# A planner's slack behind DMA landings, eight shifts in its order, and a last store from ScalarE's queue

## The chip, the cores and the metric

The kernel runs on one core of one Trainium2 chip. The time is device microseconds of one execution, and the median over repeated executions is compared. A core has five engines with instruction streams of their own: TensorE (PE, with its weight loads shown apart as PEld), VectorE (DVE), ScalarE (ACT), GpSimd (POOL) and SyncE (SP). SyncE only issues DMAs here. Engines wait for each other, and for DMAs, through semaphores.

## The reference

Two layers, each an attention block and a feed-forward block, over 2048 tokens of width 640 in bfloat16, applied twice with the same weights. The attention has 32 heads of width 20 and works in four segments of 512 tokens: softmax attention inside the segment, and a linear read from a memory `M`, `z` that earlier segments have written.

```python
for s in range(N):                       # N = 4 segments of L = 512
    logits = einsum('bhqd,bhkd->bhqk', qs, ks) * scale + mask
    a_dot = einsum('bhqk,bhkd->bhqd', softmax(logits), vs)
    pq = phi(qs)                         # t + 1 where t > 0, else exp(t)
    a_mem = einsum('bhld,bhde->bhle', pq, M) / (einsum('bhld,bhd->bhl', pq, z) + 1e-6)
    outs.append(g * a_mem + (1 - g) * a_dot)
    M, z = M + einsum('bhld,bhle->bhde', phi(ks), vs), z + sum(phi(ks))
...
x = x + A(layernorm(x)) ; x = x + relu(layernorm(x) @ w1) @ w2     # twice
```

The feed-forward block is 640 to 1728 and back.

## The kernel before

All of `x` stays in SBUF (`x_sb`). The work goes in eight segment passes, layer `a` 0 or 1 and segment `s` 0 to 3; pass number 4a + s is called the rank. A pass has these steps, each a Python generator that yields one instruction group at a time:

- `proj_ln`, `proj_one`, `proj_v`: layer norm, turn the rows by a DMA transpose (`xnT`), multiply with wq, wk, wv (L658, or L661 when the weight is split in four pieces of 32 columns), and evict to `stg` and `v_aug`.
- `spill` and `fill`: store `stg` to DRAM (`scr`, L946) and load it back as `pad`, four DMAs for a pair of head groups (L993), so that the 20 rows of a head stand at multiples of 32.
- `scores`, `exps`, `causal`: scores of four heads side by side (L1177), exponentials to `PT` on ScalarE (L1239), the diagonal masked on GpSimd (L1251).
- `apply`, `turn_pair`, `divide`: multiply `PT` by v (L1271), evict to `otu` (L1281), turn it by DMA to `otk`, and on VectorE divide by the sums: a reciprocal that waits for `otk` (L1357), a scaling (L1360), two products into `o_sb` (L1365).
- `phi_`, `turn_k`, `mem_write`, `mem_read`, `combine`: the memory. `phi_` is a VectorE step that waits for the landing of `scr` (L1020), an exponential on ScalarE (L1022) and a minimum on VectorE (L1023).
- `turn_o`, `out_proj`: turn `o_sb` to `oT` by two DMA transposes, multiply by wo, add to `x_sb` (L1393).
- `ln_b`, `ffn_rest`, `ffn`: layer norm, first product with ReLU (L1475 on VectorE or L1476 on ScalarE), second product, add to `x_sb` (L1497).
- `store`: write a tile of 128 tokens to the output (L1529). The last tile goes in three pieces of 320, 160 and 160 columns (L1525).

No order is written by hand. A planner, `Sched`, holds one stream per generator (39 of them, 0 to 38 in the order in which they are added, plus short ones that a stream spawns) and writes out the engines' instruction lists before the kernel is built. It has planned durations for every step and a planned landing time for every DMA. In each round it looks at the head of every stream, works out when it could start on its engine, and takes the one with the smallest key:

```python
key = (round(start + late), 0.5 if op.urgent else prio, self.rank[id(st[1])], n)
```

`start` is the planned start in ns, `n` the stream's number, and `late` an amount by which a step is put behind others. `_late` gives TensorE's steps such an amount when one of their inputs would be ready only just before their start: up to 400 ns (`SOFT`) behind another engine's result, and up to 1000 ns (`SOFT_DMA`) behind a DMA's landing. It does so only from the event `SOFT_FROM` on, a set of scores in the second segment of the first layer. Steps of the other engines had no such amount, and neither had the pairs of score groups, which pass through a class of their own (`Either`).

The planner only fixes the order on each engine and the semaphore waits that the data need. What happens on the chip follows from real durations: each of ScalarE, VectorE, GpSimd and SyncE does its list from front to back, so a step that waits holds all steps behind it. TensorE switches between three kinds of work: whole matmuls, row groups (scores) and column groups.

Of the kernel before, what the change touches and what calls it, by code (L numbers as in the profile page):

```python
# [38 lines left out]
class Prog:  # L39
    def __init__(self, sems):  # L40
        self.ops = {e: [] for e in ENGS}
        self.clk = dict(sems)
        self.cnt = {e: 0 for e in ["act", "dve", "pool", "pe"]}
        self.dcnt = {}
        self.K = {e: {} for e in ENGS}
        self.pos = {e: 0 for e in ENGS}
        self.info = {}
# [36 lines left out]
    def dma(self, e, fn, sem):  # L84
        self.pos[e] += 1
        self.dcnt[id(sem)] = self.dcnt.get(id(sem), 0) + 16
        tk = (sem, self.dcnt[id(sem)])
        self.ops[e].append(("op", fn, sem, 16))
        self.info[(id(sem), tk[1])] = ("dma%d" % id(sem), tk[1], dict(self.K[e]))
        return tk  # L90
# [71 lines left out]
        self.gen = gen  # L162


LONE_NS = 300.0
SWITCH_NS = 96.0
COLS_LAG = 1500.0
SOFT = 400
SOFT_DMA = 1000
SOFT_FROM = ("sc",6,4,1)  # L170
SEM_NS = 60.0
PE_MARGIN = 80.0
# [4 lines left out]
class Sched:  # L177


    def __init__(self, prog):  # L180
        self.P = prog
        self.free = {e: 800.0 for e in ENGS}
        self.t = {}
        self.events = {}
        self.streams = []
        self.dma_free = 0.0
        self.rank = {}
        self.mode = "full"
        self.landed = set()

    def add(self, prio, gen):
        self.streams.append([prio, gen, None, None, False])
        self.rank[id(gen)] = 0

    def at(self, tk):
# [2 lines left out]
    def set(self, *key, tks=()):  # L198
        assert key not in self.events, key
        self.events[key] = [t for t in tks if t is not None]  # L200
# [44 lines left out]
    def _alts(self, op):  # L245
# [17 lines left out]
            res.append((start + hold, start, k, e))  # L263
        return res

    def _late(self, op):
        late = 0.0
        if op.alts[0][0] == "pe" and SOFT_FROM in self.events:
            waits = op.waits
            if op.acq is not None:  # L270
                s = self._pick(op.acq)
                waits = waits + (s.tks if s is not None else [])
            start = max([self.free["pe"]] + [self.at(t) + SEM_NS + PE_MARGIN for t in waits])
            for t in waits:
                k = (id(t[0]), t[1])
                late = max(late, self.t[k] + SEM_NS + PE_MARGIN + (SOFT_DMA if k in self.landed else SOFT) - start)
        if not op.lag or self.mode != "full":
            return late
        waits = op.waits
        if op.acq is not None:  # L280
            s = self._pick(op.acq)
            waits = waits + (s.tks if s is not None else [])
        ready = max([self.at(t) for t in waits], default=0.0) + SEM_NS + PE_MARGIN
        return max(late, ready + op.lag - max(ready, self.free["pe"]))

    def run(self):
        while True:
            best = None
            moved = True
            while moved:  # L290
                moved = False
                for st in list(self.streams):
                    had, ended = st[2], st[4]
                    self._settle(st)
                    moved = moved or st[4] != ended
                    moved = moved or st[2] is not had
            heads = []
            for n, st in enumerate(self.streams):
                if st[4]:
                    continue  # L300
                if isinstance(st[2], Op):
                    heads.append((st[0], n, st, self._alts(st[2]), st[2], self._late(st[2])))
                elif isinstance(st[2], Either):
                    both, lone = st[2].fn()
                    if both is not None:
                        heads.append((st[0], n, st, self._alts(both), both, 0.0))
                    if lone is not None:
                        heads.append((8, n, st, self._alts(lone), lone, LONE_NS))
            for prio, n, st, alts, op, late in heads:
                ok = []  # L310
                for end, start, k, e in alts:
                    if not any(p2 < min(prio, HOLDERS) and st2 is not st
                               and any(e2 == e and s2 + HOLD_TOL[e] < end for _, s2, _, e2 in al2[:1])
                               for p2, _, st2, al2, _, _ in heads):
                        ok.append((end, start, k))
                if not ok:
                    continue
                end, start, k = min(ok)
                key = (round(start + late), 0.5 if op.urgent else prio, self.rank[id(st[1])], n)
                if best is None or key < best[0]:  # L320
                    best = (key, st, end, start, k, op)
            if best is None:
                stuck = [st for st in self.streams if not st[4]]
                if not stuck:
                    return
                raise RuntimeError("stuck: " + "; ".join(
                    str(getattr(st[2], "key", None) or [s.name for s in getattr(st[2], "slots", [])][:2]) for st in stuck))
            _, st, end, start, k, op = best
            e, hold, fns, tail = op.alts[k]
            if e == "pe":  # L330
                op.mode = self._mode(op)
                self.mode = op.mode
                if op.mode == "cols" and op.cols is not None:
                    fns = op.cols
            waits, slot = op.waits, None
            for s in op.take:
                s.free = False
            if op.acq is not None:
                slot = self._pick(op.acq)
                slot.free = False  # L340
                waits = waits + slot.tks
                fns = [(lambda eng, fn=fn, slot=slot: fn(eng, slot), mark) for fn, mark in fns]
            self.P.waits(e, waits)
            self.free[e] = end
            if op.dma is not None:
                tk = self.P.dma(e, fns[0][0], op.dma)
                self.landed.add((id(tk[0]), tk[1]))
                self.dma_free = max(self.dma_free, start + 300.0) + tail[1]
                self.t[(id(tk[0]), tk[1])] = max(self.dma_free, end) + tail[0]
                if tail[2]:  # L350
                    self.free[e] = max(end, self.dma_free)
                out = tk
            else:
                marks = []
                for fn, mark in fns:
                    tk = self.P.op(e, fn, mark)
                    if tk is not None:
                        self.t[(id(tk[0]), tk[1])] = end + tail
                        marks.append(tk)
                out = marks[0] if len(marks) == 1 else (marks or None)  # L360
            st[2], st[3] = None, ((slot, out) if slot is not None else out,)
# [52 lines left out]
def bass_interleave_layers__memory_aug_infini_attn__dense_activation_relu__prompt_kernel(  # L414
    nc, A_x, A_wq, A_wk, A_wv, A_wo, A_beta, B_x, B_w1, B_w2, out,
):
    with contextlib.ExitStack() as es:
# [3 lines left out]
        S = Sched(P)  # L421
# [1095 lines left out]
        def store(b, s):  # L1517
            if b == 0:
                return
            for i in range(NJ):  # L1520
                t = 4 * s + i
                if (s, i) == (NSEG - 1, NJ - 1):
                    for hf, c0, n in ((0, 0, 320), (1, 320, 160), (2, 480, 160)):
                        tks = yield Need("sum", b, s, 2 * i + hf)
                        S.last = yield dma("sp", dout, 256 * n, lambda e, c0=c0, n=n: e.dma_start(  # L1525
                            out[0, t * 128:(t + 1) * 128, c0:c0 + n], x_sb[:, t, c0:c0 + n]), tks)
                    return
                tks = yield Need("xB", b, s, i)
                S.last = yield dma("sp", dout, 163840, lambda e, t=t: e.dma_start(  # L1529
                    out[0, t * 128:(t + 1) * 128, :], x_sb[:, t, :]), tks)  # L1530

        dout = sem_("d_out")
# [48 lines left out]
        S.add(6, each(ffn))  # L1581
        S.add(5, each(ffn_rest))
        S.add(6, each(store))
        S.add(7, warm_pe())
        S.add(7, consts())
# [35 lines left out]
```

The softmax here doesn't subtract the row's maximum and nothing guards it: scores larger than these inputs give would overflow.

## Time and profile before

| what | us |
|---|---|
| median of 10 runs | 559.28 |
| lowest and highest of them | 557.94, 561.74 |
| the profiled execution | 561.83 |
| its span, first to last instruction | 559.9 |
| ScalarE busy | 405.8 |
| VectorE busy | 416.7 |
| GpSimd busy | 191.8 |
| exponentials L1239, 320 of them, mean 1027 ns | 309.1 |

The span is what the trace covers; the execution's own time holds some 1.9 us more around it. The profile splits the time three ways: busy time of each engine, groups of instructions by line with the idle time of the engine in front of them and what ended it, and the chain of waits, which follows the end of the run back to what released each step. The granted TensorE clock is full throughout. DMAs move 61.3 MB in all, most on SyncE's queue; each also ends in a wait of some engine, and from issue to landing the turned rows `otk` take 3.4 us in the median, `xnT` 3.8, `oT` 3.6.

### The profile page before, as it was taken

The page shows a single profiled execution, that of the slowest core. Times are in us where ns is not written, and L with a number is a line of the kernel's source. Part 1 is how long each engine was busy: PE and PEld are TensorE (multiplying, and loading weights), DVE is VectorE, ACT ScalarE, POOL GpSimd, SP SyncE. Part 2 cuts the span into 40 slices and gives each one's busy share as a digit, 9 for nine tenths or more (in the row PEclk, how much of TensorE's full clock was granted, in tenths as well). Part 3 has the DMA queues.
Part 4 walks back from the last instruction along what each step waited for, and adds up shares of the span by engine and source line. Part 5 has one row for each costly group of instructions (what it writes and reads, how often), then busy time and mean ns, then how long its engine had stood idle before and what let it go on. Part 6 is the DMA issues. An engine that isn't in the chain of part 4 may idle for free.

```text
span 559.9 us, 18928 instructions
## 1 busy us (share of the span) xinstructions
PE 547.0 (98%) x8265; PEld 308.7 (55%) x8265; DVE 416.7 (74%) x1063; ACT 405.8 (72%) x514; POOL 191.8 (34%) x302
## 2 busy tenths in 40 slices
PE   8998999999999999999999999999999999999997
PEld 7454654455554555646446554565555654666656
DVE  4967988898899798897779988889965767335102
ACT  5699889899777887797788887887865787432140
POOL 5245344333344334344433443335410433201000
PEclk9999999999999999999999999999999999999999
DMA  8595999925684148275285423872426412443101
GB/s 270 133 229 155 223 192 205 235 50 78 112 162 83 38 100 168 55 102 100 59 186 99 91 44 108 155 127 21 67 56 167 108 45 29 89 84 61 40 2 50
DMA packets 130292, 61.32 MB, mean 110 GB/s; under 512 B 109090, under 2 KB 120098, under 8 KB 130210
## 3 DMA queue, kind: packets, MB, share of 16 engines
q1 hardware_dynamic: 129792, 59.62, 49.9%
q8 instruction: 65, 1.06, 0.8%
q10 hardware_dynamic: 418, 0.49, 0.3%
q14 instruction: 17, 0.14, 0.1%
HBM read 20.57 MB, written 12.85 MB: 60 GB/s over the span
## 4 chain that ended last, share of the span: by engine, by line
PE 82%; DMA 7%; DVE 7%; ACT 2%; SPq 1%; issue 1%; POOL 0%; ACTq 0%; POOLq 0%
PE ps L658 39%; PE ps L661 24%; PE ps L1177 8%; PE ps L1271 6%; DMA otk<-otu 4%; ACT PT L1239 2%; PE ps L1310 1%; PE ps L1114 1%; PE ps L1057 1%; PE ps L635 1%; DMA xnT<-xn_tok 1%; DVE o_sb L1365 1%; DMA phk<-phs 1%; PE ps L1451 1%; DMA pad<-scr 1%
## 5 line engine op out<-in xcount | busy, mean ns | idle before, releaser
L1239 ACT ACTIVATE PT<-ps 128x1024 bf16<-128x1024 f32 x320 | 309.1, 1027 | 66.3 <-PE ps L1177 62.0
L1251 POOL TENSOR_SCALAR_AFFINE_SELECT PT<-PT 128x512 bf16<-128x512 bf16 x256 | 166.1, 666 | 268.1 <-ACT PT L1239 267.9
L658 PE MATMUL ps<-w_r,hT 128*128 128x320 bf16 x508 | 81.5, 299 | 0.0
L1497 DVE TENSOR_TENSOR x_sb<-x_sb,ps 128x320 bf16<-128x320 bf16 (+1 forms) x65 | 30.8, 474 | 55.0 <-PE ps L661 45.7
L661 PE MATMUL ps<-xnT,w_r 128*32 128x512 bf16 x1144 | 68.3, 379 | 0.5 <-issue 0.5
L1177 PE MATMUL ps<-pad 20*128 20x512 bf16 (+3 forms) x1024 | 63.4, 301 | 3.0 <-ACT PT L1239 2.1
L658 PEld LDWEIGHTS ps<-w_r,hT 128*128 128x128 bf16 x508 | 47.4, 98 | 23.7 <-issue 5.3
L658 PE MATMUL ps<-xnT,w_r 128*128 128x512 bf16 x234 | 57.9, 380 | 1.3 <-DVE hT L1475 0.9
L679 DVE BATCH_NORM_STATS2 stats<-x_sb 128x6 f32<-128x320 bf16 x124 | 55.5, 469 | 2.9 <-DMA x_sb<-in_A_x_dram 2.5
L1476 ACT ACTIVATE hT<-ps 128x512 bf16<-128x512 f32 x57 | 34.1, 599 | 23.4 <-PE ps L661 20.8
L661 PE MATMUL ps<-w_r,hT 128*32 128x320 bf16 (+1 forms) x1348 | 49.7, 294 | 0.0
L1177 PEld LDWEIGHTS ps<-pad 20*128 20x128 bf16 x1024 | 17.9, 92 | 54.6 <-issue 25.1
L661 PEld LDWEIGHTS ps<-xnT,w_r 128*32 128x32 bf16 x1144 | 29.4, 97 | 25.2 <-issue 0.7
L1281 DVE CAST otu<-ps 128x512 bf16<-128x512 f32 x51 | 34.9, 684 | 10.6 <-PE ps L1271 10.4
L1271 PE MATMUL ps<-PT,v_aug 128*21 128x128 bf16 (+3 forms) x896 | 40.5, 301 | 0.0
L661 PEld LDWEIGHTS ps<-w_r,hT 128*32 128x32 bf16 x1348 | 34.7, 97 | 8.9
L1393 DVE TENSOR_TENSOR x_sb<-x_sb,ps 128x320 bf16<-128x320 bf16 x64 | 30.0, 477 | 12.1 <-PE ps L661 8.6
L1475 DVE TENSOR_SCALAR hT<-ps 128x512 bf16<-128x512 f32 x47 | 32.2, 685 | 7.3 <-PE ps L658 5.5
L695 POOL TENSOR_TENSOR rstd<-lnU,mhalf 128x2 f32<-128x2 f32 (+2 forms) x26 | 20.6, 791 | 45.6 <-DVE lnU L691 36.0
L658 PE MATMUL ps<-wo_r,oT 128*128 128x320 bf16 x223 | 35.4, 300 | 0.4 <-DVE x_sb L1393 0.4
L658 PEld LDWEIGHTS ps<-xnT,w_r 128*128 128x128 bf16 x234 | 20.9, 97 | 25.3 <-issue 5.1
L1022 ACT ACTIVATE stg<-stg 128x512 bf16<-128x512 bf16 x50 | 31.5, 634 | 2.5 <-DVE rtmp L1020 2.2
(109 smaller groups left out, 739.6 us busy)
## 6 DMA issues: line engine op xcount, KB each, us to landing
pad<-scr SPq DMA_DIRECT2D x124, 80.0 KB
scr<-stg SPq DMA_DIRECT2D x34, 256.0 KB, 3.4
out_dram<-x_sb SPq DMA_DIRECT2D x15, 160.0 KB, 1.8
w_r<-in_B_w_dram SPq DMA_DIRECT2D x10, 216.0 KB, 2.5
w_r<-in_B_w_dram SPq DMA_DIRECT2D x13, 160.0 KB, 3.3
x_sb<-in_A_x_dram SPq DMA_DIRECT2D x10, 160.0 KB, 3.2
scr<-w_r SPq DMA_DIRECT2D x5, 256.0 KB, 3.0
wv_r<-in_A_wv_dram SPq DMA_DIRECT2D x1, 800.0 KB, 8.3
```

Of the source, the lines that this page charges most:

```text
L658: return e.matmul(view(dst.ap, b), a, b, start=(k == 0), stop=(k == last))
L661: return e.matmul(view(dst.ap[rows], b), part, b, start=(k == 0), stop=(k == last))
L679: tk = yield dve(320, 1, lambda e, c2=c2: e.bn_stats(stats6[:, t % 12, c2, :], x_sb[:, t, c2 * 320:(c2 + 1) * 320]), xt)
L1022: te = yield act(512, lambda e, q=q: e.activation(q, q, ACT.Exp), [tr] + p, psum=False)
L1177: fns.append([(lambda e, z=z, j=j, hh=hh, N=N, o=o, sl=sl, q=hh % 2: e.matmul(slot.ap[:, q, o:o + N], sl.ap[32 * hh:32 * hh + DH, z, 0, 12 ...
L1239: tx = yield act(1024, lambda e, dst=dst, src=src: e.activation(dst, src, ACT.Exp, scale=SCALE), sc + pw)
L1251: tm = yield pool(600.0, lambda e, reg=reg: e.affine_select(out=reg, in_=reg, pattern=[[0, 4], [1, 128]], compare_op=ALU.is_ge, fill=0.0, ...
L1271: fns.append((lambda e, OD, j=j, hh=hh: e.matmul(OD.ap[32 * hh:32 * hh + DH + 1, 128 * j:L], VAUG[vx(a, s)][:, j, 4 * g + hh, :], pt.ap[:, ...
L1281: te = yield evac(L, 1, lambda e: e.tensor_copy(dst, OD.ap), lambda e: e.activation(dst, OD.ap, ACT.Copy), [tk] + OTU[0].tks)
L1475: th = yield evac(512, 1, lambda e: e.tensor_scalar(hT[:, dc, :], bk.ap[:, :], 0.0, None, ALU.max), lambda e: e.activation(hT[:, dc, :], b ...
L1476: lambda e: e.activation(hT[:, dc, :], bk.ap[:, :], ACT.Relu), [tk] + HT.tks)
L1497: ta = yield dve(n, 1, lambda e: e.tensor_tensor(x_sb[:, t, c0:c0 + n], x_sb[:, t, c0:c0 + n], bk.ap[:, 0:n], ALU.add), [tk], urgent=True)
```

## The change

Four edits, all in the planner but the last.

1. `_late` now also gives an amount to steps of ScalarE, VectorE and GpSimd that are no DMAs: from `SOFT_FROM` on, a step that would start less than 1000 ns after the planned landing of a DMA it waits for is ranked as if it started at landing plus 1000 ns.
2. `_landing` does the same for pairs of score groups, behind the landing of `pad`.
3. A table `NUDGE` adds an amount in ns to the key of a stream's steps during one rank: for (stream, rank), turn_o 7, out_proj's second half 9, ln_b's second half 11, combine 14, turn_k 19, ffn_rest 33, loads 37. Ended streams are dropped from the list, so each stream now carries its number along.
4. Of the three pieces of the last tile the third is issued by ScalarE's queue instead of SyncE's.

Ranking a step later does not make it wait on the chip: it may be written behind another step in its engine's list, or stay where it was.

```diff
--- before.py
+++ after.py
@@ -162,6 +162,16 @@
         self.gen = gen
 
 
+NUDGE = {
+    (7, 2): 200,
+    (9, 2): -450,
+    (11, 5): 450,
+    (14, 2): 200,
+    (14, 7): 100,
+    (19, 6): -100,
+    (33, 2): 100,
+    (37, 0): -200,
+}
 LONE_NS = 300.0
 SWITCH_NS = 96.0
 COLS_LAG = 1500.0
@@ -183,13 +193,15 @@
         self.t = {}
         self.events = {}
         self.streams = []
+        self.count = 0
         self.dma_free = 0.0
         self.rank = {}
         self.mode = "full"
         self.landed = set()
 
     def add(self, prio, gen):
-        self.streams.append([prio, gen, None, None, False])
+        self.streams.append([prio, gen, None, None, False, self.count])
+        self.count += 1
         self.rank[id(gen)] = 0
 
     def at(self, tk):
@@ -263,6 +275,12 @@
             res.append((start + hold, start, k, e))
         return res
 
+    def _landing(self, op):
+        start = max([self.free["pe"]] + [self.at(t) + SEM_NS + PE_MARGIN for t in op.waits])
+        soft = SOFT_DMA if SOFT_FROM in self.events else 0.0
+        return max([0.0] + [self.at(t) + SEM_NS + PE_MARGIN + soft - start for t in op.waits
+                           if (id(t[0]), t[1]) in self.landed])
+
     def _late(self, op):
         late = 0.0
         if op.alts[0][0] == "pe" and SOFT_FROM in self.events:
@@ -274,6 +292,9 @@
             for t in waits:
                 k = (id(t[0]), t[1])
                 late = max(late, self.t[k] + SEM_NS + PE_MARGIN + (SOFT_DMA if k in self.landed else SOFT) - start)
+        if op.alts[0][0] != "pe" and op.dma is None and SOFT_FROM in self.events:
+            start = max([self.free[op.alts[0][0]]] + [self.at(t) + SEM_NS for t in op.waits])
+            late = max([0.0] + [self.at(t) + SEM_NS + 1000 - start for t in op.waits if (id(t[0]), t[1]) in self.landed])
         if not op.lag or self.mode != "full":
             return late
         waits = op.waits
@@ -286,6 +307,7 @@
     def run(self):
         while True:
             best = None
+            self.streams = [st for st in self.streams if not st[4]]
             moved = True
             while moved:
                 moved = False
@@ -295,7 +317,8 @@
                     moved = moved or st[4] != ended
                     moved = moved or st[2] is not had
             heads = []
-            for n, st in enumerate(self.streams):
+            for st in self.streams:
+                n = st[5]
                 if st[4]:
                     continue
                 if isinstance(st[2], Op):
@@ -303,7 +326,7 @@
                 elif isinstance(st[2], Either):
                     both, lone = st[2].fn()
                     if both is not None:
-                        heads.append((st[0], n, st, self._alts(both), both, 0.0))
+                        heads.append((st[0], n, st, self._alts(both), both, self._landing(both)))
                     if lone is not None:
                         heads.append((8, n, st, self._alts(lone), lone, LONE_NS))
             for prio, n, st, alts, op, late in heads:
@@ -316,7 +339,7 @@
                 if not ok:
                     continue
                 end, start, k = min(ok)
-                key = (round(start + late), 0.5 if op.urgent else prio, self.rank[id(st[1])], n)
+                key = (round(start + late + NUDGE.get((n, self.rank[id(st[1])]), 0)), 0.5 if op.urgent else prio, self.rank[id(st[1])], n)
                 if best is None or key < best[0]:
                     best = (key, st, end, start, k, op)
             if best is None:
@@ -1522,7 +1545,7 @@
                 if (s, i) == (NSEG - 1, NJ - 1):
                     for hf, c0, n in ((0, 0, 320), (1, 320, 160), (2, 480, 160)):
                         tks = yield Need("sum", b, s, 2 * i + hf)
-                        S.last = yield dma("sp", dout, 256 * n, lambda e, c0=c0, n=n: e.dma_start(
+                        S.last = yield dma(("sp", "sp", "act")[hf], dout, 256 * n, lambda e, c0=c0, n=n: e.dma_start(
                             out[0, t * 128:(t + 1) * 128, c0:c0 + n], x_sb[:, t, c0:c0 + n]), tks)
                     return
                 tks = yield Need("xB", b, s, i)
```

## The prediction

> **What bounds the kernel now.** I read the page's busy times and its chain first, then the table of stretches over the part whose order changes, then the weight loads in front of every pause of TensorE, then the chains that end in those pauses, and last SyncE's queue and the end.
>
> ```profile
> PE 547.0 (98%) x8265; PEld 308.7 (55%) x8265; DVE 416.7 (74%) x1063; ACT 405.8 (72%) x514; POOL 191.8 (34%) x302
> ...
> PE 82%; DMA 7%; DVE 7%; ACT 2%; SPq 1%; issue 1%; POOL 0%; ACTq 0%; POOLq 0%
> ```
>
> TensorE is the bound: busy 98% of the span, and 82% of the chain. A reordering can gain only where TensorE pauses. The instruction order of the two kernels is the same up to the 1,427th matmul, which the trace has at 119.7 us; everything before that stays. The stretches after it (columns: length, then busy time of PE, PEld, DVE, ACT, POOL, then clock, DMA share, GB/s):
>
> ```profile
> 135.00:165.00 30.00, 29.42 (x387) 16.50 (x388) 26.22 (x70) 22.13 (x25) 12.04 (x19) 1.00 0.72 129
> 165.00:200.00 35.00, 33.89 (x483) 16.57 (x471) 30.89 (x74) 28.42 (x35) 13.21 (x21) 1.00 0.33 68
> ...
> 350.00:400.00 50.00, 49.30 (x685) 27.17 (x678) 44.94 (x112) 40.41 (x51) 20.12 (x30) 1.00 0.57 98
> 400.00:430.00 30.00, 29.02 (x539) 16.41 (x537) 18.50 (x48) 18.60 (x28) 4.78 (x7) 1.00 0.41 96
> ```
>
> Length less PE: 0.58 + 1.11 + 0.70 + 0.98 = 3.4 us of pause; all other stretches from 119.9 on are full, the last 69.6 us, 487 to 556.6, among them. The modelled end of a matmul hides part of a pause, so I size each by the weight load that follows (its idle time in the bracket). Ordinary gaps there are 0.26 us before a score group and 0.23 after one:
>
> ```profile
> 148.53 0.52 PEld L658 LDWEIGHTS ps<-wo_r,oT 128*128 128x128 bf16 x5 [0.72 <-DVE x_sb L1393]
> ...
> 197.32 0.13 PEld L1177 LDWEIGHTS ps<-pad 20*128 20x128 bf16 x4 [1.15 <-issue]
> ...
> 428.18 0.10 PEld L1177 LDWEIGHTS ps<-pad 20*128 20x128 bf16 x4 [1.15 <-DMA pad<-scr]
> ```
>
> Over the ordinary gap these are 0.5, 0.9 and 0.9 us. Four more are idle 0.64 us at 153.6, 0.73 at 166.8, 1.00 at 367.9 and 0.50 at 407.1, which is 0.4, 0.5, 0.7 and 0.3 too much. Sum 4.2 us: all that a perfect order could take from this part. What starts them, at 197:
>
> ```profile
> 187.36 4.84 DMA otk<-otu
> 192.20 0.02 issue
> 192.22 0.35 DVE rden L1357
> ...
> 194.19 0.22 DVE rtmp L1020
> 194.41 0.02 issue
> 194.43 0.63 ACT stg L1022
> ```
>
> VectorE stood 1.08 us at L1357 for the turned rows `otk`; L1020 and the PSUM evictions stood behind it, ScalarE's step L1022 behind L1020, and behind that the exponentials that free the score banks (L1239, 1.83 us in the chain from 195.39). The chain to 148.5 has the same head: `otk` issued at 142.17, L1357 idle 1.28 us, then the two L1393 whose banks TensorE wants. And on SyncE:
>
> ```profile
> 420.51 2.89 SPq L701 DMA_TRANSPOSE oT<-o_sb  x2
> 423.50 1.69 SPq L993 DMA_DIRECT2D pad<-scr  x4
> ```
>
> The `pad` rows for which TensorE waits at 428.2 were issued behind 2.89 us of transposes. For the end, the line of the last three stores (shortest, median and longest issue in ns, then first and last start):
>
> ```profile
> L1525 SPq DMA_DIRECT2D out_dram<-x_sb x3: 332/332/1312, 555.2 to 557.0; - x3
> ```
>
> The first two stores took 332 ns to issue, the third 1312; the last matmul and its addition are over at 556.97, and the span ends at 559.9.
>
> **What the Trainium skill says.** "TensorE: Matmul & The Clock Gate", section "Architectural detail: the array is 16× 32×32, not 1× 128×128", says that ScalarE and VectorE work strictly in order; the chain to 197.3 agrees, one wait of 1.08 us at L1357 moved work that needs no `otk`. "TensorEngine Tiling (Array Packing)", "Key Properties", says that changing the tiling mode drains the array; the 0.26 and 0.23 us around a score group, against none inside a run, agree. "DMA: Bandwidth & Descriptors", "Issuing engines are not separate DMA queues", says that the same 16 engines carry what SyncE and ScalarE issue, and only issue time is saved. "Runtime: NRT & Kernel Launch", "Instruction fetch mechanics", has instructions fetched in 16 KiB blocks; the trace has such packets, one of 1.69 us at 556.2, under the final stores.
>
> **The change part by part.** *Work on TensorE.* I counted the new order. Eleven 512-column matmuls take 2.48 us in the chain, 0.21 each once the last one's 0.38 is off. Weighting all columns so, with four pieces of a split matmul side by side, the old order holds 489.8 us of columns and the new 489.7. Changes of mode: 334 in both. The 252 fewer matmul instructions are split groups made whole, with the same columns: nothing. So whatever is gained or lost is pauses.
>
> *Slack of 1 us for steps of VectorE, ScalarE and GpSimd behind a landing.* It adds no wait; it ranks a step that would start within 1 us of its landing's planned time behind steps that are ready. I measured the room by the columns TensorE works off between the step that an `otk` transfer comes from and the last one VectorE knows of when it reads. Over the 25 divisions in the changed part the median goes from 4.26 to 5.35 us, and those under 4.2 us from 12 to 2. VectorE's five waits at L1357 between 120 and 487 us are 4.2 us in the profile; two reached TensorE. Gone: 0.9 (197) + 0.5 (148) = 1.4 us. The others cost nothing even now, having hidden beside full PSUM banks.
>
> *The same slack for score pairs, and the table.* Score pairs are now ranked behind the landing of `pad` like other matmuls. The table moves turn_o and combine of segment 2 by +200 ns, out_proj's second half by -450, ln_b's second half of segment 5 by +450, combine of 7 by +100, turn_k of 6 by -100, ffn_rest of 2 by +100, and loads by -200 (which leaves the start as it was). These are ranks alone. What I can read off is SyncE's order: for the last segment all 16 `pad` loads now come before the `oT` pair, so the 2.89 us are no longer ahead of the one that TensorE lacked at 428: 0.9 us gone. In exchange that `oT` pair is issued later, behind loads of 0.3 to 0.4 us each. Ten ReLU evictions go from ScalarE (599 ns) to VectorE (685 ns): 6.9 us more there, covered by 143 us of idle; if the cover is gone, 0.1 us each.
>
> *The pauses left.* The one at 166.8 (0.5) hangs on `xnT`, whose least room goes from 7.05 to 6.54 us: I leave it. Those at 153.6, 368 and 407 (1.4) hang on queues of VectorE and ScalarE that are shuffled anyway; I let them be replaced by as much.
>
> *Last store from ScalarE.* ScalarE has nothing from 549 us on, so nothing is queued behind its wait. No row shows a store there; its two loads of x at the start took 392 and 443 ns to issue, its small copies 670 to 1348. Bounds: 1.0 us gained (1312 to 332), or 0.5 lost if a queue unused since 20 us starts slowly. The data still shares the engine that fetches instructions until 557.9, so I take 0.8 gained.
>
> Sum: 1.4 + 0.9 + 0.8 = 3.1 us. The profiled execution was 561.83 us (span 559.9, 1.9 around it) and would become 558.7. The median of the runs, 2.5 lower, goes from 559.28 to 556.2.
>
> **The rivals.** *More than that.* The reshuffle also clears 166.8 and the other three, and the store gains its full 1.0: 4.2 + 1.0 = 5.2, giving 554.1. For it: the stretches 200 to 350 show that this loop can run with no pause. Against: nothing in the slack addresses a pause without a DMA in its chain.
>
> *As before.* The slack works on planned times, and the plan's error is what made the pauses; new ones of some 2.5 us turn up elsewhere, and the store gains 0.3: 559.0. For it: three of five waits at L1357 were hidden, so removing waits need not move TensorE.
>
> *Slower.* Dividing later makes a segment's last `o_sb` later, and with it `oT` and the output projection. Place: the seven handovers from L1365 to L658 on `oT` in the changed part. In columns their least room goes from 6.70 to 6.28 us, and four of 14 waits lie under 7.0 instead of one. What they need: 0.5 for the sum, 2.9 for two issues, 3.6 to landing, together 7.0. If all seven run 0.7 us short, 5.0 us are lost against 3.1 gained: 561.2. It decides from 0.45 us a handover on. Against: with 6.70 us of room TensorE has no wait on `oT` today.
>
> **How the numbers follow.** Forecast 0.50, more 0.16, as before 0.21, slower 0.13. About 0.3% (1.7 us) is what a measurement of this kernel can tell from no change. The first two are faster, the third the same: 0.66, 0.21, 0.13. The likeliest alone spans 554.9 to 557.6. For 8 in 10 the range runs to 553.2, as pauses that modelled ends hide may add 0.9 to the larger gain, and up to 560.6, into the slower case. 556.2 is the likeliest.
>
> **What would show it.** Right: L1357's waits after 120 us under 1.5 us together, no weight load of scores with over 0.6 us behind `pad`, PE full in the stretches that had 1.11 and 0.98 us of pause, the last store landing under 2 us after the last addition. Wrong: new gaps of 0.7 us or more before L658 on `oT` or `xnT`, or before L1177 behind ScalarE, as many as went; then the order has moved its pauses only.

## The result, and the profile after

| | before | changed |
|---|---|---|
| median, us | 559.82 (49 runs) | 555.79 (14 runs) |
| lowest, highest | 556.89, 563.4 | 554.88, 557.58 |
| profiled execution | 561.83 | 556.05 |
| its span | 559.9 | 554.1 |

The ratio is 0.9927, with a 95% interval of 0.9913 to 0.9942: 4.0 us less. The forecast was 556.2. The changed kernel's lines stand 23 further down (L1357 is L1380, L1393 is L1416, L1177 is L1200, L1525 is L1548). In the kernels without the table, E1, E2, E4 and E7 below, they stand 14 further down (L1357 is L1371).

The page of the changed kernel, busy times and chain by engine:

```profile
PE 545.3 (98%) x8013; PEld 308.4 (56%) x8013; DVE 422.3 (76%) x1069; ACT 403.8 (73%) x508; POOL 193.8 (35%) x302
...
PE 91%; DVE 3%; ACT 2%; DMA 1%; SPq 1%; issue 0%; POOL 0%; POOLq 0%
```

DMA was 7% of the chain and is 1%; PE was 82% and is 91%. VectorE has 5.6 us more to do, and that costs nothing. The stretches that had the pauses (length, then busy time of PE and the others):

```profile
135.00:165.00 30.00, 30.00 (x378) 17.24 (x378) 26.18 (x73) 23.84 (x29) 11.77 (x19) 1.00 0.62 128
165.00:200.00 35.00, 35.00 (x506) 17.78 (x508) 33.15 (x82) 29.50 (x35) 14.66 (x21) 1.00 0.39 88
...
350.00:400.00 50.00, 49.77 (x675) 29.08 (x668) 45.64 (x123) 40.60 (x54) 19.09 (x29) 1.00 0.52 93
400.00:430.00 30.00, 30.00 (x362) 15.27 (x360) 21.80 (x48) 22.54 (x29) 8.47 (x13) 1.00 0.52 129
```

Between 119.9 and 487 us TensorE pauses 0.23 us in this profile and 3.40 us in the one before. How that came about shows at the division whose `otk` is turned at about 142 us in both kernels. VectorE in the changed kernel (start, length, step, count, idle before):

```profile
143.07 0.49 DVE L1416 TENSOR_TENSOR x_sb<-x_sb,ps 128x320 bf16<-128x320 bf16 x1 [1.26 <-PE ps L681]
144.02 0.49 DVE L1416 TENSOR_TENSOR x_sb<-x_sb,ps 128x320 bf16<-128x320 bf16 x1 [0.46 <-PE ps L681]
145.27 1.44 DVE L1416 TENSOR_TENSOR x_sb<-x_sb,ps 128x320 bf16<-128x320 bf16 x3 [0.77 <-PE ps L681]
146.66 0.35 DVE L1380 RECIPROCAL rden<-otk 128x32 f32<-128x32 bf16 x1
```

Since that transfer was issued, five additions that free PSUM banks have gone ahead of the reciprocal, the last three in the row at 145.27, and the reciprocal no longer waits. Before, three had gone ahead, VectorE stood idle 1.28 us at the reciprocal for the landing, and two such additions were queued behind it. The chain of this stretch, which held 5.27 us of DMA before, is TensorE's alone:

```profile
141.60 2.38 PE ps L681 x15
143.98 0.33 PE ps L1200 x8
144.31 2.36 PE ps L681 x16
146.67 0.33 PE ps L1200 x4
147.00 0.95 PE ps L681 x5
```

SyncE before the last segment's scores. The sixteen loads are issued in one piece, with no `oT` pair ahead of them:

```profile
409.57 1.24 SPq L724 DMA_TRANSPOSE otk<-otu  x1
410.86 3.34 SPq L969 DMA_DIRECT2D scr<-stg  x4
414.71 6.00 SPq L1016 DMA_DIRECT2D pad<-scr  x16
```

At the end, the line of the last three stores says how long their issues took (shortest, median, longest, in ns):

```profile
L1548 SPq DMA_DIRECT2D out_dram<-x_sb x2: 332/332/333, 549.8 to 550.6; - x2
L1548 ACTq DMA_DIRECT2D out_dram<-x_sb x1: 368/368/368, 551.6 to 551.6; - x1
```

The issue of 1312 ns is gone, but from the end of the last addition to the end of the span 2.54 us pass where 2.92 passed. The unchanged first part varies from execution to execution too: the 1,427th matmul comes at 118.8 us here and at 119.7 before, between 117.3 and 120.0 over the ten profiles of this document. And the execution profiled before was a slow one of its kernel, 2.0 us above the median of the 49 runs. So the spans of the two profiles differ by 5.8 us and the medians by 4.0.

### The profile page after: what moved, and what is told of

It is laid out like the page before. It is cut to its first block, busy times and chain, and to the rows that moved or that the text cites. A ratio compares the mean times of both kernels' runs of the same rounds, so it can differ in the third digit from the quotient of the medians.

```text
span 554.1 us, 18424 instructions
## 1 busy us (share of the span) xinstructions
PE 545.3 (98%) x8013; PEld 308.4 (56%) x8013; DVE 422.3 (76%) x1069; ACT 403.8 (73%) x508; POOL 193.8 (35%) x302
## 4 chain that ended last, share of the span: by engine, by line
PE 91%; DVE 3%; ACT 2%; DMA 1%; SPq 1%; issue 0%; POOL 0%; POOLq 0%
PE ps L681 45%; PE ps L684 25%; PE ps L1200 9%; PE ps L1294 6%; PE ps L1080 2%; ACT PT L1262 1%; PE ps L1333 1%; PE ps L1137 1%; PE ps L658 1%; PE ps L1474 1%; DMA pad<-scr 1%; DMA beta_bc<-in_A_beta_dram 1%; DVE xn_tok L748 0%; SPq L996 0%; DVE stg L880 0%
## 5 line engine op out<-in xcount | busy, mean ns | idle before, releaser
L681 PE MATMUL ps<-w_r,hT 128*128 128x320 bf16 x481 | 78.7, 300 | 0.0
L1200 PE MATMUL ps<-pad 20*128 20x512 bf16 (+3 forms) x1024 | 63.4, 301 | 1.9 <-ACT PT L1262 1.0
L681 PE MATMUL ps<-xnT,w_r 128*128 128x512 bf16 x270 | 65.1, 380 | 0.0
L684 PE MATMUL ps<-xnT,w_r 128*32 128x512 bf16 x1000 | 59.3, 379 | 0.2 <-issue 0.2
L684 PE MATMUL ps<-w_r,hT 128*32 128x320 bf16 (+1 forms) x1456 | 54.3, 294 | 0.0
L1200 PEld LDWEIGHTS ps<-pad 20*128 20x128 bf16 x1024 | 17.9, 92 | 53.1 <-ACT PT L1262 27.1
L1499 ACT ACTIVATE hT<-ps 128x512 bf16<-128x512 f32 x47 | 28.1, 598 | 21.6 <-PE ps L684 19.8
L684 PEld LDWEIGHTS ps<-w_r,hT 128*32 128x32 bf16 x1456 | 37.4, 97 | 10.1
L1416 DVE TENSOR_TENSOR x_sb<-x_sb,ps 128x320 bf16<-128x320 bf16 x64 | 30.1, 480 | 15.7 <-PE ps L684 8.0
L1498 DVE TENSOR_SCALAR hT<-ps 128x512 bf16<-128x512 f32 x57 | 38.6, 680 | 4.0 <-PE ps L681 2.6
L681 PEld LDWEIGHTS ps<-xnT,w_r 128*128 128x128 bf16 x270 | 24.6, 97 | 28.2 <-issue 4.2
L684 PEld LDWEIGHTS ps<-xnT,w_r 128*32 128x32 bf16 x1000 | 25.7, 97 | 21.6 <-issue 0.4
L880 DVE CAST stg<-ps 128x512 bf16<-128x512 f32 x42 | 28.6, 684 | 6.8 <-PE ps L681 6.6
```

The costliest lines, as they stand in the source:

```text
L681: return e.matmul(view(dst.ap, b), a, b, start=(k == 0), stop=(k == last))
L684: return e.matmul(view(dst.ap[rows], b), part, b, start=(k == 0), stop=(k == last))
L880: te = yield evac(N, 1, lambda e: e.tensor_copy(sg.ap[:, t0:t0 + N], bk.ap[:, 0:N]), lambda e: e.activation(sg.ap[:, t0:t0 + N], bk.ap[:, ...
L1200: fns.append([(lambda e, z=z, j=j, hh=hh, N=N, o=o, sl=sl, q=hh % 2: e.matmul(slot.ap[:, q, o:o + N], sl.ap[32 * hh:32 * hh + DH, z, 0, 12 ...
L1416: ta = yield dve(320, 1, lambda e: e.tensor_tensor(x_sb[:, t, 320 * hf:320 * hf + 320], x_sb[:, t, 320 * hf:320 * hf + 320], bk.ap[:, 0:32 ...
L1498: th = yield evac(512, 1, lambda e: e.tensor_scalar(hT[:, dc, :], bk.ap[:, :], 0.0, None, ALU.max), lambda e: e.activation(hT[:, dc, :], b ...
```

## The experiments

Two theories went in. "Room": VectorE waits for `otk` in front of work that needs no `otk`; the slack puts that work ahead, and the rest of the change matters little. "Lucky draw": the order is so entangled that any change shuffles the pauses, and the full combination, the table above all, is a good draw. The four edits were run alone and then left out one at a time. Each ratio is to runs of the kernel before that were made together with the variant, one set for E1 to E4 and another for E5 to E8. With all four switched off, the changed program has exactly the order of the kernel before.

### E1: the slack alone

```diff
+NUDGE = {}
...
+        if op.alts[0][0] != "pe" and op.dma is None and SOFT_FROM in self.events:
+            late = max([0.0] + [self.at(t) + SEM_NS + 1000 - start for t in op.waits if (id(t[0]), t[1]) in self.landed])
...
                     if both is not None:
                         heads.append((st[0], n, st, self._alts(both), both, 0.0))
```

> The kernel before with the slack for VectorE, ScalarE and GpSimd steps alone; no table, no slack for score pairs, last store on SyncE. In its order the divisions with under 4.2 us of TensorE work between the source of otk and the reading step are 1 of 25 (12 before, 2 with the whole change); column work and mode changes come to 0.9 us more than before. Theory 'room' (the gain comes from VectorE no longer standing at L1357 before the turned rows land): the waits on otk after 120 us fall under 1 us, those pauses of TensorE go, -1.4 us for them, +0.9 for the mode changes, other pauses as before: 559.3 against 559.8, at best -2. Theory 'lucky draw' (any reshuffle moves the pauses, and only the full combination is a good one): waits and pauses of 3 to 4 us elsewhere, 560 to 562.

Measured: 557.53 us median, ratio 0.9969 (0.9953 to 0.9986). Its waits of VectorE between 120 and 487 us (us in all, times, longest), and a stretch that had 1.11 us of pause:

```profile
DVE rden L1371 <- DMA otk<-otu: 0.3, 1, 0.3
```

```profile
165.00:200.00 35.00, 35.00 (x485) 17.63 (x484) 31.76 (x72) 29.35 (x37) 14.66 (x22) 1.00 0.43 83
```

The waits went from 4.2 us to 0.3 and TensorE's pauses in that part from 3.40 to 0.48, in spite of 0.9 us more of work and mode changes. "Room" is borne out and "lucky draw", with 560 to 562, is not. The size was underrated: "room" had 0.5 us gained, at best 2, and 1.7 came, as pauses that it let stand went as well.

### E2 and E3: the score pairs alone, the table alone

```diff
-                        heads.append((st[0], n, st, self._alts(both), both, 0.0))
+                        heads.append((st[0], n, st, self._alts(both), both, self._landing(both)))
```

> The slack for score pairs behind pad alone. 14 of 25 divisions keep under 4.2 us of room; work and mode changes +0.9 us. Theory 'room': VectorE's waits on otk stay at 3 to 5 us after 120 us; only the pause on pad at 428 (0.9) may go: 559 to 560.5. Theory 'lucky draw': anywhere from 558 to 562, with no tie to the waits on otk.

Measured: 559.02 us, ratio 0.9994 (0.9980 to 1.0008). No gain. Its order is that of the kernel before up to about 345 us, so the chain before its largest pause, 0.59 us at 194, is the known one with numbers of its own (start, length, what):

```profile
184.16 4.76 DMA otk<-otu
188.92 0.02 issue
188.94 0.35 DVE rden L1371
...
191.14 0.63 ACT stg L1036
...
192.10 1.83 ACT PT L1253 x2
193.93 0.14 issue
194.07 0.40 PE ps L1191 x4
```

The table alone:

```diff
+NUDGE = {
+    (7, 2): 200,
...
+    (37, 0): -200,
+}
```

> The table of eight shifts alone. 15 of 25 divisions keep under 4.2 us of room; work and mode changes +1.3 us. Theory 'room': no gain, 560 to 562, waits on otk stay at 3 us or more. Theory 'lucky draw', in the form that the table picks a good order: 1 to 3 us gained.

Measured: 559.97 us, ratio 1.0014 (1.0003 to 1.0026): a little slower, if anything. A stretch that was full before has pauses of 1.28 us in all, and just ahead of the largest (0.66 us at 322.3) stands VectorE's wait:

```profile
300.00:350.00 50.00, 48.72 (x739) 25.93 (x739) 43.12 (x112) 41.02 (x52) 20.78 (x32) 1.00 0.45 75
```

```profile
321.59 0.35 DVE L1380 RECIPROCAL rden<-otk 128x32 f32<-128x32 bf16 x1 [1.27 <-DMA otk<-otu]
```

So shuffling does move pauses, as the rival says, but they appear at the same kind of wait as before. In E2, E3 and E5 single waits of 5.8 to 6.2 us show at about 415 us too; they reach TensorE little (0 to 0.3 us of pause from 400 to 430 us in E2 and E3), so the sum of waits, 9.5 to 11.3 us in these three where 3 to 5 were expected for E2, is no measure by itself.

### E4 and E8: the store alone, and the change without it

```diff
-                        S.last = yield dma("sp", dout, 256 * n, lambda e, c0=c0, n=n: e.dma_start(
+                        S.last = yield dma(("sp", "sp", "act")[hf], dout, 256 * n, lambda e, c0=c0, n=n: e.dma_start(
```

> Only the last of the three final stores on ScalarE's queue; every other instruction stands as before. Forecast had 0.8 us, bounds 1.0 gained and 0.5 lost. The trace of the whole change has 2.57 us from the last addition to the end of the span against 2.93 before. If that difference is the queue: -0.4 us, 559.4 against 559.8. If the issue of 1312 ns alone was the loss: -1.0. If the block of instructions on the shared DMA engine sets the end: 0.

> The whole change with the last store left on SyncE; every other instruction stands as in the whole change. If the queue is worth the 0.36 us between the two traces: 556.2 against 555.8 of the whole change. If the long issue of 1312 ns comes back: 556.8. If nothing: 555.8.

Measured: alone 559.56 us, ratio 1.0006 (0.9991 to 1.0021); without it 555.93 us, ratio 0.9941 (0.9920 to 0.9963), beside 0.9927 with it. The store is worth nothing that these runs can tell, and a gain of 0.8 us lies outside the interval of E4. E8, with all three stores on SyncE, has one long issue again:

```profile
L1548 SPq DMA_DIRECT2D out_dram<-x_sb x3: 332/332/782, 550.0 to 551.7; - x3
```

and its span is 554.1 us, the same as that of the whole change. The long issue is not what the end waits for. Nor does SyncE's queue bring it about by itself: in E2, with the same three stores on SyncE, no issue is long.

```profile
L1539 SPq DMA_DIRECT2D out_dram<-x_sb x3: 332/332/332, 551.6 to 553.3; - x3
```

### E5, E6 and E7: the change without one part

```diff
-        if op.alts[0][0] != "pe" and op.dma is None and SOFT_FROM in self.events:
+        if False:
```

> The whole change without the slack for VectorE, ScalarE and GpSimd steps. 13 of 25 divisions have under 4.2 us of room; work and mode changes +1.3 us against before. Theory 'room': the gain of 4 us is lost, 559 to 561, VectorE waits on otk 3 us or more. Theory 'lucky draw': unknown, but not tied to the slack; some 2 us of gain may stay.

Measured: 559.33 us, ratio 1.0007 (0.9992 to 1.0023). Without the slack for the other engines the whole gain is gone, table, pairs and store all in place.

```diff
-                        heads.append((st[0], n, st, self._alts(both), both, self._landing(both)))
+                        heads.append((st[0], n, st, self._alts(both), both, 0.0))
```

> The whole change without the slack for score pairs. 3 of 25 divisions under 4.2 us; work and mode changes as before. Theory 'room': most of the gain stays, 556 to 557.5; a pause on pad may come back (0.9 us; least room of pad 6.26 us against 7.17). Theory 'lucky draw': any other order than the one chosen has pauses of 3 to 4 us again, 558.5 to 560.

Measured: 556.36 us, ratio 0.9952 (0.9934 to 0.9971). Most of the gain stays, though VectorE waits 3.1 us on `otk`, 2.9 of them at once at 416 us, and the pause on `pad` does come back, smaller:

```profile
428.24 0.10 PEld L1200 LDWEIGHTS ps<-pad 20*128 20x128 bf16 x4 [0.65 <-DMA pad<-scr]
```

```diff
-NUDGE = {
-    (7, 2): 200,
...
-}
+NUDGE = {}
```

> The whole change without the table of eight shifts. 5 of 25 divisions under 4.2 us; work and mode changes as before. Theory 'room': 556 to 557.5, the table adds 1 us or less. Theory 'lucky draw', with the table as the pick: 558.5 to 560.

Measured: 555.16 us, ratio 0.9936 (0.9918 to 0.9955). The table adds nothing that shows beside 0.9927; "room" had expected 556 to 557.5.

All ten kernels together. "Short" is the number of divisions, of 25, with under 4.2 us of room, read from the order as in the prediction. "Work" is an estimate of columns and mode changes against the kernel before, with 0.13 us for each change (from start to start the traces show 0.10 to 0.11 us over the columns). The pauses are length less PE busy from 119.9 to 487 us, and "changed part" is the time from the start of the 1,427th matmul to the start of the last one, both in one profile each.

| kernel | slack | short | work, us | pauses, us | changed part, us | ratio |
|---|---|---|---|---|---|---|
| before | no | 12 | 0 | 3.40 | 436.6 | 1 |
| E4 store alone | no | 12 | 0 | 1.76 | 434.6 | 1.0006 |
| E2 pairs alone | no | 14 | +0.9 | 1.04 | 435.0 | 0.9994 |
| E3 table alone | no | 15 | +1.3 | 2.37 | 437.0 | 1.0014 |
| E5 all but slack | no | 13 | +1.3 | 1.67 | 436.0 | 1.0007 |
| E1 slack alone | yes | 1 | +0.9 | 0.48 | 433.5 | 0.9969 |
| E6 all but pairs | yes | 3 | 0 | 0.32 | 432.4 | 0.9952 |
| E7 all but table | yes | 5 | -0.1 | 0.41 | 432.6 | 0.9936 |
| E8 all but store | yes | 2 | -0.1 | 0.23 | 432.2 | 0.9941 |
| whole change | yes | 2 | -0.1 | 0.23 | 432.2 | 0.9927 |

The five with the slack have 0.2 to 0.5 us of pauses, the five without it 1.0 to 3.4; the changed part takes 432.2 to 433.5 us with it and 434.6 to 437.0 without, and the ratios part in the same way. The part ahead of it, which is the same in all, takes 118.8 us on average with the slack and 118.9 without. The waits on `otk` do not part the kernels so: they sum to 2.8 us in E4 and to 3.1 in E6. What counts is whether a late landing reaches TensorE.

That can be watched, since the five kernels without the slack have one order up to about 160 us. The `otk` transfer issued at about 142 us landed after 5.27, 5.09 and 5.17 us in the kernel before, E3 and E5; VectorE waited 1.28, 1.09 and 1.17 us for it, and TensorE paused 0.43 us in front of the same matmul in all three. In E4 and E2 it landed after 4.61 and 4.54 us, VectorE waited 0.62 and 0.55 us, and there is no pause. E4's wait, and the weight load that was idle 0.72 us before:

```profile
146.97 0.35 DVE L1371 RECIPROCAL rden<-otk 128x32 f32<-128x32 bf16 x1 [0.62 <-DMA otk<-otu]
...
148.20 0.52 PEld L672 LDWEIGHTS ps<-wo_r,oT 128*128 128x128 bf16 x5 [0.23 <-DVE x_sb L1407]
```

At 197 us, where the kernel before, E2 and E4 still have one order, waits of 1.08 and 1.01 us cost TensorE 0.68 and 0.59 us, and one of 0.84 us cost nothing. So the old order had some reserve for a late landing, and too little for the slowest (3.0 to 5.5 us for `otk` before); the slack adds to it.

The column of work accounts for part of why the slack alone gives less than half of the gain: its order costs 0.9 us more in work and mode changes. That cost is gone in E7, which adds the pairs, and in E6, which adds the table in their place, so the runs do not show that it takes the pairs.

Not measured: the slack for L1357 alone or for all steps but it, a later planned landing of `otk` in its place, and other amounts than 1000 ns. Their orders can be counted all the same: with the slack for score pairs and L1357 alone 3 of 25 divisions are short, with that for score pairs and all steps but L1357 14, and with `otk` planned to land 1000 ns later in the kernel before 2. By that count the room comes from where the reciprocal is placed, and a later planned landing would place it as well. What these orders take on the chip is open.

## Why the prediction was right

*That TensorE's pauses are all there is to win* held. Columns and mode changes were counted as equal, and the time from the first changed matmul to the last one fell from 436.6 to 432.2 us with as much work in it. That the 4.2 us sized by weight loads come so close to the 4.0 that the medians gained is in part luck. They were sized in one slow execution; E4, with the same order, has 1.76 us of pauses instead of 3.40, and its changed part takes 434.6 us, only 2.4 more than that of the whole change.

*The slack, 1.4 us for the pauses at 148 and 197:* shown, by E1 and E5 from both sides. Both pauses are absent in all five kernels that have the slack; without it the one at 148 is there in three profiles of five. Their price is that of a slow landing, not of every execution.

*The `pad` loads, 0.9 us:* the pause at 428 went, and SyncE's order is as read. But SyncE's order alone does not decide it. E3 has the `oT` pair ahead of the loads, as before, and no pause there; E1 has no `oT` pair ahead of them and still waits for `pad` at 422.7 us (0.51 us of idle); in E6 the pause returns at 0.65 us of idle.

*The pauses left, 1.9 us, which the forecast let stand or be replaced:* this term was mis-sized. At 153.6, 166.8, 368 and 407 nothing of note came in their place; the largest idle time of TensorE left in that part is 0.2 us. They are also gone in E1 and E7, so it does not take the table. Nor does it take the slack for each: the one at 166.8 is missing in E2, which still has the old order there, and those at 368 and 407 are gone in E3 and E5 too, where pauses of 1.28 and 1.09 us came between 300 and 350 us in their place. That is the exchange which the forecast had assumed; with the slack none came. The step "nothing in the slack addresses a pause without a DMA in its chain" was too strict. By which route the slack keeps new ones away was not traced.

*The store, 0.8 us:* wrong, it is 0 (E4 and E8). The step that failed took the long issue of 1312 ns for time on the path. The Trainium skill ("DMA: Bandwidth & Descriptors", "Issuing engines are not separate DMA queues") has it that only issue time is saved, and the runs show that here not even that was on the path: in E8 the third store took 782 ns to issue and landed at 553.70 us, in the whole change 368 ns, and it landed at 553.66. The sign named for this term did not come either: the last store lands 2.1 us after the last addition, not under 2.

The two errors, 1.9 us too little and 0.8 too much, come to about the 0.9 us between 3.1 forecast and 4.0 measured. That they cancel in part is luck: the number came closer than its terms.

*The rivals.* "More than that" was right that the other four pauses go, and wrong on the store. "As before" described the table, the pairs and the store taken singly. "Slower" did not show: the changed part's waits of TensorE hold none on `oT` or `xnT`, though the least room of `oT` is 6.28 us instead of 6.70. So 6.3 us of room were enough in this profile, and the need of 7.0 was put too high.

## What to carry to other kernels

Where an engine works its list in order, a step that waits for a DMA costs what is queued behind it, not its own wait: put ready work that frees buffers ahead of it, with a reserve for slow landings. When several edits of an order come together, run each alone and each left out; here no gain came without one of the four, that one alone gave less than half, and a table with eight tuned numbers added nothing that shows to the other three. A pause that hangs on how fast a transfer lands is not the same in every execution, so size it from more than one profile. Before a long issue of a DMA is given a price, see whether the landing moves with it.

## What the runs showed of the hardware

The pauses of one order differ from one execution to the next by more than the change's single terms: 3.40 and 1.76 us in the profiles of the kernel before and E4, with the landing of one `otk` transfer at about 147 us shifting its reader by 0.5 us. The runs of the whole change scatter less than those of the kernel before (standard deviation 0.7 us against 1.4), but E3 without the slack has 0.9 and E8 with it 1.0, so that this comes from the slack is not shown.

The Trainium skill ("Runtime: NRT & Kernel Launch", "Instruction fetch mechanics") has the fetch of 16 KiB blocks mostly hidden. The trace before shows where one may not be: a block took 1.69 us from 556.2 us on, and some rows of the first of the last stores moved only from 557.93 on. The changed kernel has such a fetch at the same place (550.7 us, 1.51 us). The ten profiles agree with it: where the block was in before the last addition was over (E2 and E5), the span ends 1.9 and 2.0 us after that addition; in the other eight, where the block is in 0.4 to 1.1 us after it, the span ends 2.3 to 2.9 us after, by and large the later the block, the later the end. The queue of the last store makes no such difference. No run moved the fetch, so that it sets the end is not shown.
